# Seven more zero products on TensorE between the products of units 0 and 1

## The chip, the cores and the metric

The kernel runs on one core of one Trainium2 chip. Times are device microseconds of one execution; the time of a kernel is the median of its runs. The engines named here are TensorE (PE in the profile, with its weight loads as PEld), VectorE (DVE), ScalarE (ACT), GpSimd (POOL) and SyncE (SP), which issues nearly all DMAs.

## The reference

Two stages follow each other. The first is a linear attention with a decaying state, for 4 batches of 8 heads, 768 time steps and 48 channels:

```python
for t in range(S):
    cur = einsum('bhd,bhe->bhde', u[None] * kt, vt)
    y[:, :, t] = einsum('bhd,bhde->bhe', rt, state + cur)
    state = wt[:, :, :, None] * state + einsum('bhd,bhe->bhde', kt, vt)
```

The second mixes the tokens of each batch: with `x` the heads of `y` side by side (768 x 384), `wq = x @ w_q`, `wk = x @ w_k` (64 columns each), `W_tok = wq @ wk.T / 8`, and the output is `relu(W_tok @ x) @ w_out`.

## The kernel before, in words

The time axis is cut into units of 256 steps, two chunks of 128 each; 4 batches of 3 units make 12 units. For a unit the kernel loads w, k, r and v (each 384 KB; the v of the last batch in four pieces). GpSimd, ScalarE or VectorE cast them to bf16. ScalarE takes the logarithm of w (`lw`, line 407); TensorE sums it along time with a triangular matrix (`CM,lw`); ScalarE's exponentials of that are `ep` (447) and `en` (454). TensorE transposes k and r (`PM,k`, `PM,r`); VectorE or ScalarE copies the turned k as `ks`. VectorE and GpSimd form `RT` = r times ep (516), `KT` = k times en (521, 526) and `qT` = r times k (506). TensorE's `RT,KT` products are the scores within a chunk; VectorE masks them into `AM` (595). `UB,qT` gives the diagonal part, copied as `dd`, from which GpSimd forms `Vd` (575). `v,PM` puts v in order (copied as `VB`). KT is transposed back (`ID,KT`, copied as `kd`), and `VB,kd` with the old state through `SB,IDU` gives the next state, which VectorE scales into `SB` (658). `VB,AM` and `SB,RT` add up to y, which VectorE turns into `X` (710). The second stage's products (`XT`, `QK`, `TS`, `MX`, `wo`) follow at the end of each batch.

Nothing is scheduled by the compiler. The program first makes a list of steps (`Plan.add`), each a group of instructions on one engine, and then gives them out in the order of the list `ORDER` (lines 82 to 122), a permutation of the steps' numbers. `WAYS` names the engine where there is a choice, and `BANKS` (129) names the PSUM bank of each PSUM buffer, in the order in which the buffers are made. PSUM has eight banks, taken by many buffers in turn: a step that writes a bank must wait for the engines that last read it, and those waits follow from the order. Each engine takes its instructions strictly in the order of the list.

A zero product is a matmul of a tile of zeros, `Z` (128 x 512, set by line 250), with itself: a full-array product of 512 columns whose result nobody reads. Eighteen are issued at the start, while the first loads are on their way (251). Twelve more are steps of the plan, made at its end, each with a PSUM bank of its own from `BANKS`:

```python
for x in range(WARM):
    z = bank()
    add(("z", x), "E", lambda e, z=z: mm(at(z), Z[:, ds(0, C)], Z), [], z, [z])
```

All matmuls go through the helper `mm`, so that in the profile every TensorE instruction has its line, 179.

Of the kernel before, what the change touches and what calls it, by code (L numbers as in the profile page):

```python
# [32 lines left out]
class Plan:  # L33
# [47 lines left out]

ORDER = [
# [40 lines left out]
]  # L123
WAYS = (
    "PDDDAPPDDdPADPPDDEEEAAPPAdPAAPEAcEEAAPPAPPADPeDEEDAAAAAAAAPPDPDADPeAcEEDAPPAdPAAPEAEEEDA"
# [1 line left out]
    "DPPAPeAcceAAPPDPPPAPPAEEDDAEDADAAADAAAADADDA"  # L127
)
BANKS = [
# [6 lines left out]
]  # L136


WARM = 12


@with_exitstack
def kernel(
# [170 lines left out]
    def bank():  # L314
        return Buf("s")
# [537 lines left out]
    for n in range(N):  # L853
        if n % NU == 0:
            batch = {"k": [], "q": [], "x": []}
        unit(n, batch)
    for x in range(WARM):
        z = bank()
# [35 lines left out]
```

## Time and profile before

| | |
|---|---|
| median of 3 runs | 100.75 us (100.47 to 102.29) |
| profiled execution | 101.37 us |
| its span, first to last instruction | 99.6 us |
| TensorE busy | 86.6 us (87%), 1906 product rows |
| VectorE busy | 84.9 us (85%) |
| ScalarE busy | 79.0 us (79%) |
| GpSimd busy | 69.5 us (70%) |
| DMA | 24.68 MB, mean 248 GB/s |
| zero products | 8.4 us in 25 rows, of 30 issued |

The span is cut on the page into 40 slices of 2.5 us, with a digit for the busy share of each engine in tenths. The chain of waits goes back from the last instruction, at each step to what released it. Rows of a timeline join equal instructions that follow each other: start, length, engine, line, operation, output and inputs with their shapes, how many, and in brackets the idle time of the engine ahead of them and what ended it. A row's length goes from the first start to the last end; products are pipelined, so a following row can start before that end. Some product rows can be missing: five of the thirty zero products are.

### The profile page before, as it was taken

How to read it: one execution, taken by the hardware profiler on the slowest of the kernel's cores; microseconds unless marked ns; L12 is line 12 of the kernel's file. 1: busy time of each engine (PE TensorE's matmuls, PEld its weight loads, DVE VectorE, ACT ScalarE, POOL GpSimd, SP SyncE). 2: the span in 40 equal slices, each digit the busy share in tenths (PEclk: the TensorE clock that was granted, in tenths of full speed). 3: DMA queues.
4: the chain of work that ended last, by engine and by line, in shares of the span. 5: the costliest groups of instructions: out<-in, count | busy, mean ns of one | idle time of the engine just before them, and what ended most of it. 6: DMA issues, size and time to landing. Idle time of an engine off the chain costs nothing.

```text
span 99.6 us, 4492 instructions
## 1 busy us (share of the span) xinstructions
PE 86.6 (87%) x1906; PEld 63.3 (64%) x1911; DVE 84.9 (85%) x154; ACT 79.0 (79%) x135; POOL 69.5 (70%) x82
## 2 busy tenths in 40 slices
PE   5978796879886998999999999889998999999930
PEld 1325473756774767777776777759787687776610
DVE  6284999799979999979999999999999799783740
ACT  6034998799996799899999998999899766666920
POOL 6866354999799895799999989498996392500000
PEclk9999999999999999999999999999999999999999
DMA  1999999799999999999999977998993056030794
GB/s 17 313 327 349 324 337 296 195 295 335 289 314 298 225 311 329 344 321 268 271 330 305 316 114 218 251 156 201 282 417 115 7 210 264 10 158 7 277 367 149
DMA packets 45141, 24.68 MB, mean 248 GB/s; under 512 B 31552, under 2 KB 43968, under 8 KB 45120
## 3 DMA queue, kind: packets, MB, share of 16 engines
q1 hardware_dynamic: 44960, 24.19, 84.0%
q8 instruction: 15, 0.25, 0.9%
q10 hardware_dynamic: 160, 0.20, 0.5%
q14 instruction: 6, 0.05, 0.1%
HBM read 19.66 MB, written 4.72 MB: 245 GB/s over the span
## 4 chain that ended last, share of the span: by engine, by line
PE 37%; DVE 23%; SPq 20%; DMA 7%; issue 7%; ACT 3%; ACTq 0%; DVEq 0%
PE PS L179 37%; SPq L232 9%; SPq L237 8%; DMA vg<-in_v_dram 7%; DVE AM L595 7%; DVE X L710 6%; DVE RT L516 3%; SPq L355 2%; DVE qT L506 2%; DVE ks L333 2%; DVE SB L658 1%; ACT VB L327 1%; SPq L357 1%; ACT MX L339 1%; DVE kd L335 1%
## 5 line engine op out<-in xcount | busy, mean ns | idle before, releaser
L595 DVE TENSOR_TENSOR AM<-PS,US 128x1024 bf16<-128x1024 f32 x24 | 28.8, 1218 | 0.7 <-PE PS L179 0.7
L526 POOL TENSOR_TENSOR KT<-ks,en 128x1024 bf16<-128x1024 bf16 (+1 forms) x10 | 19.7, 1965 | 4.7 <-DVE ks L333 3.3
L575 POOL TENSOR_TENSOR Vd<-VB,dd 128x768 bf16<-128x768 bf16 (+1 forms) x14 | 18.1, 1293 | 4.5 <-ACT dd L327 3.4
L454 ACT ACTIVATE en<-PS 128x1024 bf16<-128x1024 f32 (+1 forms) x14 | 12.5, 907 | 3.0 <-PE PS L179 2.9
L179 PEld LDWEIGHTS <-KT 48*128 48x128 bf16 (+1 forms) x312 | 9.7, 94 | 6.6 <-issue 4.5
L447 ACT ACTIVATE ep<-PS 128x512 bf16<-128x512 f32 (+1 forms) x28 | 13.7, 555 | 0.1
L179 PE MATMUL PS<-wo,MX 128*128 128x384 bf16 x72 | 13.5, 327 | 0.0
L710 DVE SCALAR_TENSOR_TENSOR X<-PS,gx,Vd 128x384 bf16<-128x384 f32 x22 | 12.5, 609 | 0.7 <-PE PS L179 0.6
L407 ACT ACTIVATE lw<-wg 128x768 bf16<-128x768 f32 x12 | 10.3, 857 | 2.9 <-DMA wg<-in_w_dram 2.9
L179 PE MATMUL PS<-RT,KT 48*128 48x128 bf16 x192 | 9.7, 218 | 1.2 <-ACT VB L327 0.4
L327 ACT COPY os<-PS 128x768 f32<-128x768 f32 (+1 forms) x11 | 7.9, 714 | 3.5 <-PE PS L179 3.5
L418 POOL CAST k<-kg 128x768 bf16<-128x768 f32 x10 | 8.3, 827 | 2.5 <-DMA kg<-in_k_dram 2.5
L179 PE MATMUL PS<-Z 128*128 128x512 bf16 x25 | 8.4, 461 | 1.4 <-DVE Z L250 1.2
L418 POOL CAST r<-rg 128x768 bf16<-128x768 f32 x10 | 8.2, 825 | 1.6 <-DMA rg<-in_r_dram 1.6
L179 PEld LDWEIGHTS <-MX 128*128 128x128 bf16 x72 | 6.5, 97 | 3.6 <-DVE MX L341 0.2
L516 DVE TENSOR_TENSOR RT<-PS,ep 128x1024 bf16<-128x1024 bf16 (+1 forms) x14 | 8.4, 605 | 0.0
L179 PE MATMUL PS<-VB,AM 128*128 128x48 bf16 x192 | 8.0, 184 | 0.4 <-issue 0.4
L506 DVE TENSOR_TENSOR qT<-PS,ks 128x1024 bf16<-128x1024 bf16 x12 | 8.2, 684 | 0.1
L339 ACT ACTIVATE MX<-PS 128x768 bf16<-128x768 f32 (+1 forms) x12 | 8.0, 682 | 0.4
L179 PE MATMUL PS<-CM,lw 64*128 64x128 bf16 x192 | 7.4, 217 | 0.5 <-DVE AM L595 0.3
L327 ACT CAST VB<-PS 128x768 bf16<-128x768 f32 x8 | 6.4, 804 | 1.1 <-PE PS L179 0.6
L179 PEld LDWEIGHTS <-AM 128*128 128x128 bf16 x192 | 6.3, 96 | 1.6 <-issue 0.7
(90 smaller groups left out, 191.9 us busy)
## 6 DMA issues: line engine op xcount, KB each, us to landing
kg<-in_k_dram SPq DMA_DIRECT2D x12, 384.0 KB, 6.4
wg<-in_w_dram SPq DMA_DIRECT2D x12, 384.0 KB, 5.0
rg<-in_r_dram SPq DMA_DIRECT2D x12, 384.0 KB, 5.8
vg<-in_v_dram SPq DMA_DIRECT2D x9, 384.0 KB, 6.3
out_dram<-os SPq DMA_DIRECT2D x9, 384.0 KB, 2.5
vw<-in_v_dram SPq DMA_DIRECT2D x4, 288.0 KB, 6.7
out_dram<-os SPq DMA_DIRECT2D x5, 192.0 KB, 2.4
wof<-in_moe_w_out_dram SPq DMA_DIRECT2D x1, 576.0 KB, 6.2
```

What stands on the lines that cost most here:

```text
L179: return nc.tensor.matmul(o, l, rr, start=start, stop=stop, skip_group_check=True, is_transpose=trans)
L327: nc.scalar.copy(o, i)
L407: nc.scalar.activation(view(lw.tile, 0, [[64, H], [512, 2], [1, D]]), view(g["wg"].tile, 0, [[D2, H], [D, 2], [1, D]]), ACT.Ln, bias=0.0, ...
L418: op(view(o.tile, 0, [[64, NP], [256, 4], [1, D]]), view(g[src].tile, 0, [[2 * D2, NP], [D, 4], [1, D]]))
L447: nc.scalar.activation(view(ep.tile, cs[0] * NP * EW + off, [[EW, NP * len(cs)], [step, 2], [1, 32]]), view(at(cw), cs[0] * 512 + j * 64, ...
L454: nc.scalar.activation(en.tile[:, ds(cs[0] * 512, w_)], at(cw)[:, ds(cs[0] * 512, w_)], ACT.Exp, bias=0.0, scale=-1.0)
L506: lambda e: nc.vector.tensor_tensor(plain(qT.tile), turned(512), plain(ks.tile), ALU.mult),
L516: nc.vector.tensor_tensor(plain(RT.tile, cs, 32), turned(512, cs, True), plain(ep.tile, cs, EW // 4), ALU.mult)
L526: x.tensor_tensor(KT.tile[:, cols], ks.tile[:, cols], en.tile[:, cols], ALU.mult)
L575: (nc.vector if e == "D" else nc.gpsimd).tensor_tensor(Vd.tile[:, cols], VB.tile[:, cols], view(dd.tile, cs[0] * H, [[1, len(cs) * H], [0, ...
L595: AMs[c] = add(("AM", n, c), "D", lambda e, c=c, A=A: nc.vector.tensor_tensor(view(AM[c].tile, 0, [[C, 8], [1, C]]), view(at(A), 0, [[C, 8 ...
L710: nc.vector.scalar_tensor_tensor(view(X.tile, 2 * i * DM + hh * D, [[D2, H], [1, D]]), view(at(y), hh * 512, [[D, H], [1, D]]), gx, view(V ...
```

## The change

The number of zero products in the plan goes from 12 to 19. The seven new steps have the numbers 734 to 740; they are put into `ORDER` at five places between the products of units 0 and 1, and `BANKS` gets seven more entries, one for each: 4, 0, 0, 1, 0, 0, 2. The order of all other steps, their engines and their banks stay. The lists are written out with other line breaks, and the file is one line longer, so that a line of the kernel before has a number one higher in the changed one.

```diff
-    14, 30, 18, 19, 727, 79, 80, 81, 38, 33, 40, 32, 729, 82, 83, 84, 35, 731, 37, 39, 43, 726,
+    14, 30, 18, 19, 727, 79, 80, 81, 38, 33, 40, 32, 729, 82, 83, 84, 35, 731, 37, 39, 734, 43,
...
-WARM = 12
+WARM = 19
```

How TensorE's instructions stand, with the engine whose semaphore an instruction waits for: `LDWEIGHTS` loads the stationary operand, `MATMUL` is the product; the numbers in the names are those of the buffers (`_101` and `_99` are of unit 0, `_102` and `_100` of unit 1). First the end of unit 1's k transposes, unit 0's first score products and the first product with `qT`. Before:

```order
L179 LDWEIGHTS k_1_90
L179 MATMUL PS<-PM,k_1_90 128x2x32
L179 LDWEIGHTS KT_101 [waits DVE_49]
L179 MATMUL PS<-RT_99,KT_101 128x128 [waits Activation_49]
...
L179 LDWEIGHTS qT_97 [waits DVE_49]
L179 MATMUL PS<-UB,qT_97 128x2
```

The same place in the changed kernel:

```order
L180 LDWEIGHTS k_1_90
L180 MATMUL PS<-PM,k_1_90 128x2x32
L180 LDWEIGHTS Z
L180 MATMUL PS<-Z 128x512 [waits DVE_49]
L180 LDWEIGHTS Z
L180 MATMUL PS<-Z 128x512
L180 LDWEIGHTS KT_101
L180 MATMUL PS<-RT_99,KT_101 128x128 [waits Activation_49]
...
L180 LDWEIGHTS qT_97
L180 MATMUL PS<-UB,qT_97 128x2
```

Two zero products into bank 0 stand ahead of the score products. The first of them waits for VectorE, and neither the score products nor the products with `qT_97` do so any more: the wait of the latter has moved ahead of the former.

The second place is between unit 0's second score products and unit 1's first. Before:

```order
L179 LDWEIGHTS KT_101
L179 MATMUL PS<-RT_99,KT_101 128x128
L179 LDWEIGHTS Z
L179 MATMUL PS<-Z 128x512 [waits DVE_49]
L179 LDWEIGHTS Z
L179 MATMUL PS<-Z 128x512
L179 LDWEIGHTS KT_102 [waits DVE_49]
L179 MATMUL PS<-RT_100,KT_102 128x128 [waits Activation_49]
```

In the changed kernel:

```order
L180 LDWEIGHTS KT_101
L180 MATMUL PS<-RT_99,KT_101 128x128
L180 LDWEIGHTS Z
L180 MATMUL PS<-Z 128x512 [waits Activation_49]
L180 LDWEIGHTS Z
L180 MATMUL PS<-Z 128x512 [waits DVE_49]
L180 LDWEIGHTS Z
L180 MATMUL PS<-Z 128x512
L180 LDWEIGHTS Z
L180 MATMUL PS<-Z 128x512 [waits DVE_49]
L180 LDWEIGHTS KT_102
L180 MATMUL PS<-RT_100,KT_102 128x128
```

The first and the last of the four zero products are new, and they have taken over both waits of unit 1's score products.

The third place is ahead of the product that carries the state of unit 0 on. Before:

```order
L179 LDWEIGHTS r_1_88
L179 MATMUL PS<-PM,r_1_88 128x2x32
L179 LDWEIGHTS IDU
L179 MATMUL PS<-SB_115,IDU 128x192 [waits DVE_49]
L179 LDWEIGHTS kd_83
L179 MATMUL PS<-VB_105,kd_83 128x48
```

In the changed kernel:

```order
L180 LDWEIGHTS r_1_88
L180 MATMUL PS<-PM,r_1_88 128x2x32
L180 LDWEIGHTS Z
L180 MATMUL PS<-Z 128x512 [waits DVE_49]
L180 LDWEIGHTS IDU
L180 MATMUL PS<-SB_115,IDU 128x192
L180 LDWEIGHTS kd_83
L180 MATMUL PS<-VB_105,kd_83 128x48
```

The wait for VectorE has moved from that product to the zero product ahead of it. The remaining two new products wait for nothing: one beside the zero product that follows unit 0's r transposes, one ahead of unit 1's products with `qT_98`. The other engines' instructions stand as before.

89 rows, old and new, of tables (BANKS, ORDER) are left out of this document.

## The prediction

> **What bounds the kernel now.** I read the page first, then the chain of waits, then the timelines of TensorE, VectorE, ScalarE and GpSimd from 4 to 30 us, because all seven new products stand there. The two lines of the page are TensorE's granted clock in 40 slices and the chain's shares by engine; the rows under them are pieces of the chain (start, length, what).
>
> ```profile
> PEclk9999999999999999999999999999999999999999
> PE 37%; DVE 23%; SPq 20%; DMA 7%; issue 7%; ACT 3%; ACTq 0%; DVEq 0%
> ```
>
> ```profile
> 0.78 0.44 SPq L232
> ...
> 20.89 0.60 SPq L237
> 21.49 0.04 issue
> 21.53 7.07 DMA vg<-in_v_dram
> 28.60 0.02 issue
> 28.62 0.04 DVE v L333
> ```
>
> The clock is full in every slice. Up to 28.6 us the chain is not an engine at all: SyncE's load issues from 0.78 us on, and then the load of v for unit 3, issued at 21.53 and landed at 28.60. Only from 28.62 us on is it VectorE and TensorE that carry the end. The new products lie between 9.7 and 17.6 us, so the question is how late they make VectorE at 28.62 us, and whether any engine reaches that point late.
>
> The rows of TensorE around the seven places (start, length from the first start to the last end, product, how many; in brackets its idle time and what ended it):
>
> ```profile
> 1.23 3.57 PE L179 MATMUL PS<-Z 128*128 128x512 bf16 x8 [1.23 <-DVE Z L250]
> ```
>
> ```profile
> 4.62 2.34 PE L179 MATMUL PS<-Z 128*128 128x512 bf16 x10
> ```
>
> ```profile
> 9.74 0.39 PE L179 MATMUL PS<-Z 128*128 128x512 bf16 x1
> 10.32 0.60 PE L179 MATMUL PS<-ID,KT 48*128 48x48 bf16 x16 [0.20 <-DVE KT L526]
> 10.86 0.36 PE L179 MATMUL PS<-v,PM 64*64 64x384 bf16 x4
> 11.15 0.52 PE L179 MATMUL PS<-PM,k 64*128 64x64 bf16 x16
> 12.12 0.40 PE L179 MATMUL PS<-RT,KT 48*128 48x128 bf16 x8 [0.45 <-ACT VB L327]
> 12.45 0.35 PE L179 MATMUL PS<-UB,qT 128*128 128x2 bf16 x8
> 12.66 0.36 PE L179 MATMUL PS<-VB,kd 128*128 128x48 bf16 x8
> 12.95 0.62 PE L179 MATMUL PS<-CM,lw 64*128 64x128 bf16 x16
> 13.76 0.41 PE L179 MATMUL PS<-PM,r 64*128 64x64 bf16 x16 [0.19 <-ACT ks L327]
> 14.16 0.24 PE L179 MATMUL PS<-SB,IDU 128*128 128x192 bf16 x1
> 14.25 0.36 PE L179 MATMUL PS<-VB,kd 128*128 128x48 bf16 x8
> 14.45 0.38 PE L179 MATMUL PS<-Z 128*128 128x512 bf16 x1
> 14.76 0.36 PE L179 MATMUL PS<-v,PM 64*64 64x384 bf16 x4
> 15.04 0.35 PE L179 MATMUL PS<-UB,qT 128*128 128x2 bf16 x8
> 15.68 0.40 PE L179 MATMUL PS<-RT,KT 48*128 48x128 bf16 x8 [0.28 <-ACT dd L327]
> 16.01 0.39 PE L179 MATMUL PS<-Z 128*128 128x512 bf16 x1
> 16.55 0.40 PE L179 MATMUL PS<-RT,KT 48*128 48x128 bf16 x8
> 17.52 0.26 PE L179 MATMUL PS<-PM,k 64*128 64x64 bf16 x6 [0.57 <-POOL k L418]
> ```
>
> **What one zero product costs.** Ten follow each other from 4.62 us: (2.34 - 0.39) / 9 = 0.22 us each, where 0.39 is one's own length (row at 16.01). The eight before them took (4.62 - 1.23) / 8 = 0.42 each, at the lower clock. One that is followed by products of another tile shape delays them by 0.31 (14.45 to 14.76, and 15.68 + 0.33 = 16.01 for what precedes it). So I take 0.22 when a full-array product follows, 0.31 when a narrower one does; the bounds are 0.22 and 0.39 (no overlap at all with what follows).
>
> **The seven, one after the other.** The releasing rows on VectorE, ScalarE and GpSimd:
>
> ```profile
> 10.98 0.68 DVE L506 TENSOR_TENSOR qT<-PS,ks 128x1024 bf16<-128x1024 bf16 x1
> ...
> 12.62 1.22 DVE L595 TENSOR_TENSOR AM<-PS,US 128x1024 bf16<-128x1024 f32 x1
> 13.77 0.35 DVE L658 TENSOR_TENSOR SB<-PS,ep 128x192 bf16<-128x192 f32 x1
> ...
> 15.75 0.68 DVE L516 TENSOR_TENSOR RT<-PS,ep 128x1024 bf16<-128x1024 bf16 x1
> 16.35 2.35 DVE L595 TENSOR_TENSOR AM<-PS,US 128x1024 bf16<-128x1024 f32 x2
> 19.32 1.14 DVE L710 SCALAR_TENSOR_TENSOR X<-PS,gx,Vd 128x384 bf16<-128x384 f32 x2 [0.62 <-PE PS L179]
> ```
>
> ```profile
> 14.54 1.09 ACT L447 ACTIVATE ep<-PS 128x512 bf16<-128x512 f32 x2
> 15.50 0.19 ACT L327 COPY dd<-PS 128x16 f32<-128x16 f32 x1
> ```
>
> ```profile
> 16.64 0.82 POOL L418 CAST k<-kg 128x768 bf16<-128x768 f32 x1 [1.47 <-DMA kg<-in_k_dram]
> ```
>
> ```profile
> 28.62 1.31 DVE L333 CAST v<-vg 128x768 bf16<-128x768 f32 x1 [0.73 <-DMA vg<-in_v_dram]
> ```
>
> Product 1 stands beside the zero product at 9.74. The two take 0.22 + 0.31, so the transposes of KT can start at 10.27; they wait for KT until 10.32 anyway. Cost 0.
>
> Products 2 and 3 stand ahead of unit 0's first RT,KT products (12.12), in an idle gap of 0.45. But they write bank 0, which VectorE's qT reads until 10.98 + 0.68 = 11.66; the wait that the later UB,qT products had has moved up to product 2. A release takes about 0.05 (ep ends at 14.54 + 1.09 = 15.63, the RT,KT products that need it start at 15.68): start 11.71, then 0.22 + 0.31, and RT,KT at 12.24 in place of 12.12: +0.12. VectorE's first mask product AM follows, 12.74 for 12.62, and ScalarE's en (which waits for CM,lw) is 0.12 late too. The r transposes at 13.76 wait for ScalarE's ks, and stay.
>
> Product 4 waits for the same SB as the SB,IDU product behind it (SB ends 13.77 + 0.35 + 0.12 = 14.24). It starts at 14.29, SB,IDU at 14.51: +0.35. It fills no wait, it stands after one. The VB,kd products behind it end at 14.25 + 0.36 + 0.35 = 14.96, VectorE's next SB follows at 15.01, about 0.12 late, and so does all of VectorE's row up to the AM at 16.35.
>
> Product 5 stands ahead of UB,qT (15.04) and waits for nothing: 0.35 + 0.22 = +0.57, at 15.61. ScalarE's dd follows UB,qT's end: 15.61 + 0.35 + 0.05 = 16.01, done at 16.20. RT,KT of unit 0's second chunk has cover here, the wait for ep (14.54 + 1.09 = 15.63): 15.61 + 0.21 (12.45 to 12.66) + 0.1 for the change of shape (0.31 against 0.22) = 15.92 for 15.68, +0.24.
>
> Products 6 and 7 stand around the two zero products from 16.01 (one row of the two is missing in the trace). Product 6 waits for that dd: 16.25. The two old ones follow at 16.47 and 16.69, product 7 at 16.91 (it waits for RT, which ends at 15.75 + 0.68 + 0.12 = 16.55), and RT,KT of unit 1 at 17.22 for 16.55: **+0.67**, the largest lag of TensorE. Its AM, second of the pair at 16.35, starts at 17.22 + 0.40 + 0.05 = 17.67 for 16.35 + 2.35 - 1.22 = 17.48: +0.19 on VectorE.
>
> **Where it is taken back.** Three idle times stand behind this. TensorE's next work, the k transposes at 17.52, waits for GpSimd's cast, which itself waited 1.47 us for a DMA (16.64 + 0.82 = 17.46): TensorE is free again at 17.22 + 0.33 = 17.55, so 0.67 shrinks to 0.03. VectorE idles 0.62 before X at 19.32, which waits for TensorE: the 0.19 is gone. And at 28.62 VectorE idles 0.73 for the load of v. Between 0.78 and that load's issue at 21.53 the chain holds nothing but issues of loads, no engine, so a lag of some tenths on an engine moves none of it. Sum on the path: 0.00 to 0.05 us. Against the profiled execution (99.6 us span, 101.37 us in all, 1.77 outside) that is 101.4; the median of the runs shown is 100.75, 0.62 lower, so 100.8 on that scale.
>
> If every zero product cost its whole 0.39 with nothing overlapped, the same walk gives RT,KT of unit 1 at about 18.1, k transposes at 18.46 (+0.94) and X at 20.3 (+0.94 on VectorE); the 0.73 at 28.62 leaves 0.2 to 0.3. That is the upper end of the working: 101.05.
>
> **A gain?** The stretch itself, by a view of engines in windows (busy, instructions, granted clock, DMA share, GB/s):
>
> ```profile
> 13.40:16.80 3.40, 2.78 (x63) 1.79 (x56) 3.31 (x8) 3.40 (x7) 1.16 (x3) 1.00 1.11 324
> ```
>
> TensorE has the full clock here, and the longest idle time in the rows above is 0.57. Zero products could only raise a clock that is low; by these rows their gain is 0. [...]
>
> **Rivals.** (1) *The clock falls in executions other than the profiled one, and the new products hold it.* For it: the three runs lie between 100.47 and 102.29, wide for one kernel. Against it: full clock in all 40 slices. Price: a low stretch as long as the first one (1.23 to 4.62, 3.4 us) does half the work; of 2.78 us busy it does 1.70, so TensorE falls back by 1.08. The idle times of 0.62 and 0.73 take 1.35, so one such stretch costs nothing at the end; two cost 2.16 - 1.35 = 0.81. The change would win that: 99.9. Chance 0.10. [...]
>
> (2) *The lag gets past the covers (slower).* Place: VectorE's X at 19.32 and its cast at 28.62. It decides once VectorE is over 0.62 late before X and over 0.73 late at the cast. Against it: by the walk above it is 0.19 late. For it: behind X VectorE has no idle time that would take a lag back (third pair of the row: busy 5.00 of 5.00 us),
>
> ```profile
> 20.00:25.00 5.00, 4.14 (x102) 3.11 (x103) 5.00 (x9) 4.84 (x9) 4.92 (x4) 1.00 1.04 316
> ```
>
> so what X brings stays, up to 25 us at the least. Price +0.2 to +0.3: 101.05. Chance 0.15. At the far end of the same rival nothing covers, and 7 x 0.31 = 2.2 us come out at the end: 102.95; chance 0.04 of its own, since it needs the load of v to move with the engines.
>
> (3) The forecast, within 0.1 of 100.8: 0.71.
>
> **How the numbers follow.** Likeliest case: 100.8. A measurement of this kernel can tell about 2% from no change: below 98.7 or above 102.8. No case with a price lies below 98.7; I leave 0.03 there for rival 1 at more than two low stretches, and 0.05 above 102.8, for the far end of rival 2 and the spread of the runs. Same: 0.92. For the range, the cases' prices (99.9 to 101.05) are widened by half the spread of the runs shown, (102.29 - 100.47) / 2 = 0.91, on the upper side, where a median of few runs can fall: 101.05 + 0.91, about 102.0. Below, the lowest price and the median less that spread agree (99.9 and 99.84): 99.8.
>
> **What would show it.** In the changed kernel's timelines: the first RT,KT near 12.25; SB,IDU near 14.5; the second UB,qT near 15.6; unit 1's first RT,KT near 17.2; then k transposes still near 17.5, X near 19.3 with its idle time cut from 0.62 to about 0.4, and the cast of v at 28.6 still behind a DMA with about 0.7 idle. Wrong are the steps if X comes after 19.6, wrong is the cover if the cast waits for an engine, and wrong is the whole forecast if the load of v lands at another time or a slice of the clock falls below 9.

## The result, and the profile after

| | kernel before | changed kernel |
|---|---|---|
| median, 6 executions each | 100.69 us (100.21 to 102.29) | 102.32 us (101.69 to 103.01) |
| ratio, 95% interval | | 1.0146 (1.0097 to 1.0194) |
| profiled execution, its span | 101.37, 99.6 us | 101.69, 100.0 us |

By the medians the changed kernel is 1.6 us slower; by the two profiled executions 0.3 us. The profiled execution of the changed kernel is its fastest, that of the kernel before slower than five of its six others. Ratios here and below leave out disturbed executions, while the medians are over all, so that the two need not agree.

First the clock and the chain's shares on the page of the changed kernel:

```profile
PEclk9999999999999999999999999999999999999999
PE 49%; DVE 17%; DMA 8%; POOL 8%; issue 8%; ACT 5%; SPq 1%; DVEq 0%; ACTq 0%; POOLq 0%
```

The clock is full, as before. The first 28 us of the chain are no longer SyncE's issues: the 20% of SPq have gone to engines, TensorE first. The timeline of TensorE at the new products (start, length, product, count):

```profile
12.20 0.40 PE L180 MATMUL PS<-RT,KT 48*128 48x128 bf16 x8
14.47 0.24 PE L180 MATMUL PS<-SB,IDU 128*128 128x192 bf16 x1
15.57 0.34 PE L180 MATMUL PS<-UB,qT 128*128 128x2 bf16 x8
16.18 1.04 PE L180 MATMUL PS<-Z 128*128 128x512 bf16 x4
17.15 0.40 PE L180 MATMUL PS<-RT,KT 48*128 48x128 bf16 x8
17.39 0.41 PE L180 MATMUL PS<-PM,k 64*128 64x64 bf16 x16
```

and VectorE's X and cast of v:

```profile
19.18 1.14 DVE L711 SCALAR_TENSOR_TENSOR X<-PS,gx,Vd 128x384 bf16<-128x384 f32 x2 [0.29 <-PE PS L180]
28.40 0.73 DVE L334 CAST v<-vg 128x768 bf16<-128x768 f32 x1 [0.64 <-DMA vg<-in_v_dram]
```

Every place stands within 0.07 us of the forecast (12.24, 14.51, 15.61, 17.22), and both covers are there: the k transposes start at 17.39, not later than before, X keeps 0.29 us of its idle time, and the cast of v still waits for its load, 0.64 us. X and the cast are even 0.14 and 0.22 us earlier than before. The local walk holds; what the profiled execution lost it lost later. From 30 to 67 us VectorE is 0.8 to 1.1 us ahead of before (the cast of v took 0.73 us, 1.31 before); then ScalarE waits for a load. SyncE's issues and ScalarE's logarithm of w for unit 10 in the changed kernel:

```profile
57.84 1.52 SPq L233 DMA_DIRECT2D wg<-in_w_dram  x1
65.77 0.84 ACT L408 ACTIVATE lw<-wg 128x768 bf16<-128x768 f32 x1 [1.01 <-DMA wg<-in_w_dram]
```

and in the kernel before:

```profile
58.74 1.25 SPq L232 DMA_DIRECT2D wg<-in_w_dram  x1
65.42 0.88 ACT L407 ACTIVATE lw<-wg 128x768 bf16<-128x768 f32 x1
```

The load was issued 0.9 us earlier and came 1.7 us later (landing 65.69 for 64.00). So the lead of 0.8 us was lost to a load, and VectorE was 0.18 us late behind it; a longer wait of TensorE near 77 us (rows below) made it 0.37, and so it stayed to the end. That accounts for the profiled pair. It doesn't explain 1.6 us between the medians, and the experiments are about that.

### The profile page after: what moved, and what is told of

It is laid out like the page before. It is cut to its first block, busy times and chain, and to the rows that moved or that the text cites. A ratio compares the mean times of both kernels' runs of the same rounds, so it can differ in the third digit from the quotient of the medians.

```text
span 100.0 us, 4511 instructions
## 1 busy us (share of the span) xinstructions
PE 88.7 (89%) x1918; PEld 63.7 (64%) x1918; DVE 84.7 (85%) x154; ACT 79.2 (79%) x135; POOL 70.1 (70%) x82
## 4 chain that ended last, share of the span: by engine, by line
PE 49%; DVE 17%; DMA 8%; POOL 8%; issue 8%; ACT 5%; SPq 1%; DVEq 0%; ACTq 0%; POOLq 0%
PE PS L180 49%; DMA wg<-in_w_dram 8%; DVE X L711 5%; DVE AM L596 5%; ACT ep L448 2%; POOL KT L527 2%; POOL v L334 2%; ACT en L455 1%; DVE qT L507 1%; DVE ks L334 1%; DVE kd L299 1%; POOL US L287 1%; POOL CM L269 1%; DVE SB L659 1%; ACT lw L408 1%
## 5 line engine op out<-in xcount | busy, mean ns | idle before, releaser
L180 PE MATMUL PS<-Z 128*128 128x512 bf16 x37 | 12.3, 445 | 1.3 <-DVE Z L251 1.2
L334 DVE COPY ks<-PS 128x1024 bf16<-128x1024 bf16 x8 | 5.5, 685 | 2.3 <-PE PS L180 2.3
L180 PEld LDWEIGHTS <-Z 128*128 128x128 bf16 x37 | 3.8, 111 | 5.7 <-issue 3.0
```

What stands on the lines that cost most here:

```text
L180: return nc.tensor.matmul(o, l, rr, start=start, stop=stop, skip_group_check=True, is_transpose=trans)
L334: x.tensor_copy(o, i)
```

## The experiments

Five comparisons, each on one chip with 18 to 36 executions of the kernel before. Beside the ratio, executions are sorted by their mean granted clock: "full" is 0.99 or more.

**First comparison: parts of the change.** The kernel before on this chip: 102.47 us, 36 executions, the clock under 0.99 in 23.

A copy of the kernel before, for the size of a difference that means nothing (edit: one blank line).

> The kernel before with one blank line more, so the same instructions. Both theories expect a ratio of 1.000 within 0.003. It says how far two equal programs lie apart, which the 1.5% of the change has to be seen against; and it gives a second trace of the kernel before, in which the load of w for the last unit is expected to land near 64 us, as in the first one (64.0), and not near 65.7 as in the changed kernel.

102.75 us, ratio 0.9957 (0.9902 to 1.0012). The clock was under 0.99 in 6 of 12, so falls of the clock belong to the program as it was. In the copy's trace the load of w for unit 10, expected near 64 us, landed at 65.90: a late landing isn't the changed kernel's alone.

The seven new products with 8 columns in place of 512:

```diff
+        w_ = 512 if x < 12 else 8
-        add(("z", x), "E", lambda e, z=z: mm(at(z), Z[:, ds(0, C)], Z), [], z, [z])
+        add(("z", x), "E", lambda e, z=z, w_=w_: mm(at(z)[:, ds(0, w_)], Z[:, ds(0, C)],
+                                                    Z[:, ds(0, w_)]), [], z, [z])
```

> The seven new products stand where they stand in the changed kernel, with their waits and weight loads, but with 8 columns in place of 512. Theory A (TensorE's time: the 0.2 to 0.3 us of each new product are what costs) expects nearly the time of before, under +0.4 us. Theory B (the instructions: 14 more of them in TensorE's stream move the places where it stands still for its code) expects the loss to stay, +1.2 to +2.0 us. Theory C (the load stream is what the kernel hangs on, and any small change of the early timing shifts it) expects some other amount, 0 to +1.6.

101.92 us, 0.994 (0.9889 to 0.9991); clock under 0.99 in 7 of 12.

Products 1 to 3 alone, then 4 to 7 alone (the other numbers taken out of `ORDER`; `WARM` is 15 and 16, here the first):

```diff
-WARM = 19
+WARM = 15
```

> Only the first three of the seven new products (the one beside the zero product after the r transposes, the two ahead of unit 0's first score products). Theory A: under half of the loss, 0 to +0.5 us, since only 0.1 us of lag comes from these. Theory B: about three sevenths of it or all of it, by the places of the stalls. Theory C: anything between 0 and +1.6, and not the difference to the run with the other four.

> Only the last four of the seven new products (ahead of SB,IDU, ahead of unit 1's products with qT, and the two ahead of unit 1's score products). Theory A: nearly the whole loss, +1.0 to +1.6 us, since the 0.67 us of lag at unit 1's score products comes from these. Theory B: about four sevenths or all. Theory C: anything, and the sum with the run of the first three need not give +1.6.

The first three: 101.62 us, 0.9969 (0.9926 to 1.0012), clock under 0.99 in 1 of 12. The last four: 101.87 us, 0.9973 (0.9922 to 1.0023), 5 of 12. No part gives anything like 1.5%: theory B misses with the products of 8 columns, theory A with the last four. But the clock does fall in executions of the kernel before, as rival 1 had it. The granted clock of the unchanged copy's profiled execution, and its stretch of 3.4 us (busy times and counts of PE, PEld, DVE, ACT, POOL; clock; DMA share; GB/s):

```profile
PEclk9999967999999999589999999999999999999999
13.25:16.65 3.40, 3.40 (x62) 2.51 (x62) 3.07 (x7) 2.88 (x6) 1.69 (x3) 0.50 1.08 323
```

Half speed from 13.23 to 16.64 us, where the forecast's row for the kernel before had 1.00, and once more from 40.53. Its X still comes at 19.38 us (19.32 in the full-clock execution): one stretch here is covered, as rival 1 priced it.

**Second comparison: the changed kernel again, fewer loads, no zero products.** The kernel before: 102.64 us, 29 executions, 21 under 0.99.

> The changed kernel once more, beside the kernel before on one chip. Three theories stand. Products: the seven new products themselves cost TensorE and VectorE time that comes out at the end; then the ratio is again near 1.015 (1.010 to 1.019) at any chip. Loads: the local work keeps its covers, and what made the changed kernel 1.5% slower is when the loads of unit 10 land (w at 65.69 us in the changed kernel's trace, at 64.00 in that of before), which differs from execution to execution; then the ratio is between 0.99 and 1.005, and the profiled span goes with the landing of w of unit 10: near 99.5 if it lands before 64.5, near 100 to 101 if it lands after 65.5. Clock: the new products keep TensorE's clock from falling (6 of 6 executions of the changed kernel at 0.994 or more, 23 of 36 of the kernel before below 0.99 in the first comparison); then no more than 2 of its executions are below 0.99, and the ratio is 0.98 to 1.00 wherever the kernel before falls.

101.86 us, ratio 1.0002 (0.9947 to 1.0057), clock under 0.99 in 3 of 12. The 1.5% didn't come back.

The loads of v for units 4 to 8 left out of the kernel before, and of the changed kernel (these units then compute with old data):

```diff
+            skip = name == "vg" and n >= 4
-            g[name + "L"] = dma((name, n), lambda e, ap=ap, f=f, x=g[name].tile: f(b, i, x, ap),
+            g[name + "L"] = dma((name, n), lambda e, ap=ap, f=f, x=g[name].tile, skip=skip:
+                                None if skip else f(b, i, x, ap), buf=g[name])
```

> The kernel before without the loads of v for units 4 to 8 (the casts then read v of earlier units, so these units' outputs are wrong by that); 5 of 48 loads and 1.9 MB less, some 6.5 us of the loads' time. Loads: r and w of unit 10 land some 5 us earlier than 62.08 and 64.00, ScalarE's lw of unit 10 waits for no DMA, and the time is 0 to 1 us less than before, with a narrower spread. Products: nothing changes, ratio 0.995 to 1.005.

> The changed kernel with the same loads of v left out (units 4 to 8 read v of earlier units). To be set against the kernel before with the same loads left out. Loads: with the loads of unit 10 out of the way the two are equal within 0.5%. Products: the changed one is 1.0 to 1.9% slower than its counterpart, as it was with all loads.

100.28 us, 0.9865 (0.9816 to 0.9913), and 101.39 us, 0.9984 (0.994 to 1.0028), of the kernel before with all loads. Against each other 1.1%: the load theory, which expected them equal, was wrong, or something else lay in between. The fall of 1.4% for the kernel before is more than the 0 to 1 us that it allowed.

The twelve zero products of the plan taken out:

```diff
-WARM = 12
+WARM = 0
```

> The kernel before without its own twelve zero products in the plan (the eighteen at the start stay). Clock: the clock falls in nearly every execution (11 or 12 of 12 below 0.99, against about two thirds of those of the kernel before), over a longer stretch after 13 us, and the time is 1 to 3 us more. Products: twelve products of 0.22 to 0.39 us less, so 0 to 1 us faster. Loads: between 0.99 and 1.01.

106.2 us, 1.0304 (1.0187 to 1.0421), under 0.99 in 6 of 6, half speed from 13.11 to 30.18 us:

```profile
PEclk9999955555579957999999999999999999999995
```

So what the twelve zero products do in this kernel is to hold the clock, and that is worth 3 to 4 us (106.2 for 102.64).

**What makes the executions differ at the full clock.** The page of the kernel before had "issue 7%" in its chain, and the forecast passed over it. Of these 6.8 us most stand ahead of VectorE's, SyncE's and ScalarE's instructions; 1.2 us are TensorE waiting for nothing that the profile shows. TensorE's waits of this kind come to 1.6 us in all, and but for two of 0.15 and 0.16 us they stand at fixed places. Counting products from 0, these are among the numbers 96, 224, 352 and so on, every 128th; with its weight load each product is two instructions (the page counts 1906 products and 1911 weight loads), so every 256 instructions. The page has a queue of instructions (packets, MB, share):

```profile
q8 instruction: 15, 0.25, 0.9%
```

15 packets of 16 KB, as many as there are such places, 96 to 1888. From these counts the author takes each packet for the next block of 256 instructions of TensorE, and these places for the blocks' edges; no row names what a packet holds. Edge 1632 in the kernel before:

```profile
76.54 0.29 PE L179 MATMUL PS<-PM,k 64*128 64x64 bf16 x8
77.34 0.29 PE L179 MATMUL PS<-PM,k 64*128 64x64 bf16 x8 [0.51 <-issue]
```

and in the changed kernel:

```profile
76.72 0.20 PE L180 MATMUL PS<-PM,k 64*128 64x64 bf16 x1
77.61 0.39 PE L180 MATMUL PS<-PM,k 64*128 64x64 bf16 x15 [0.69 <-issue]
```

The same edge stands after 8 of the 16 transposes before, after 1 of them now: seven products earlier in the work, by the seven that were put in ahead. So the change does a second thing that the forecast didn't see: it moves the later block edges. Where TensorE waited at such an edge, in any of the traces, it went on 1.2 to 1.7 us after the last packet had arrived (at edge 1632 the packets arrived at 76.01 us before and at 76.44 us now).

**Third comparison: are the moved edges what costs?** The kernel before: 102.21 us, 35 executions, 18 under 0.99. The two kernels without v again, and between them the kernel before without v, with seven products of 8 columns at the start, which move the edges by as much and put nothing between units 0 and 1:

```diff
         for _ in range(18):
             mm(PS[:, ds(0, 512)], Z[:, ds(0, C)], Z)
+        for _ in range(7):
+            mm(PS[:, ds(0, 8)], Z[:, ds(0, C)], Z[:, ds(0, 8)])
```

> The kernel before without the loads of v for units 4 to 8 (wrong in these units by that), once more, as the base of the next two. If its 100.28 us against 102.64 for the kernel before was the loads' doing, it is again 1 to 2% faster than the kernel before. Code theory: TensorE's instructions arrive in blocks of 128 products, the block edges show as waits for nothing at products 480, 736, 864, 992, 1248 and 1632 of the traces so far, 0.3 to 1.5 us each, ended 1.3 to 1.6 us after a packet of 16 KB; such a packet is late when loads are in its way. Then this kernel's sum of such waits is under 1.2 us.

> The changed kernel without the same loads of v. The first pair gave 101.39 against 100.28, 1.1% more, where the load theory expected no difference. Products: again 0.7 to 1.5% more than its counterpart. Code: the same, by block edges that lie 7 products earlier in the work. Chance: within 0.5%.

> The kernel before without the same loads of v, with seven products of 8 columns more at the very start, behind the eighteen zero products of the start: they move every block edge of TensorE's code 7 products earlier in the work, as the seven new products do, and put nothing between units 0 and 1. Code: as the changed kernel without these loads, within 0.5% of it, and 0.7 to 1.5% slower than its counterpart. Products: as the kernel before without these loads, within 0.4%. Chance: all three alike.

> The changed kernel with all loads on another occasion. If the 1.5% of the first comparison belongs to the change, the ratio is 1.010 to 1.019; by the second comparison, with both kernels' executions at the full clock only, 0.995 to 1.007. Clock: no more than 4 of its executions under 0.99, more than half of those of the kernel before.

Before without v: 101.28 us, 0.9974 (0.9914 to 1.0034), with the clock low in 10 of 12 (1 to 2% under the kernel before was expected); the changed kernel without v: 100.84 us, 0.9924 (0.9865 to 0.9983), low in 1; the shift without v: 100.71 us, 0.9955 (0.9895 to 1.0015), low in 1. As medians the order of the first pair is turned round, by the clock. At the full clock, both occasions together, they are 100.07, 101.05 and 100.73 us (standard errors 0.13, 0.17, 0.21). The shift alone lies two thirds of the way to the changed kernel, against the products theory, though this rests on 9, 21 and 11 executions that the clock has picked. TensorE around 50 us in the changed kernel without v, first occasion:

```profile
50.22 0.36 PE L180 MATMUL PS<-PM,r 64*128 64x64 bf16 x13 [0.62 <-issue]
```

second occasion:

```profile
50.24 0.36 PE L180 MATMUL PS<-PM,r 64*128 64x64 bf16 x13 [0.64 <-issue]
```

and in the shift:

```profile
50.26 0.36 PE L179 MATMUL PS<-PM,r 64*128 64x64 bf16 x13 [0.64 <-issue]
```

The same wait at the same product (992); of the two traces of the kernel before without v one has 0.15 us there, in its weight loads, and one none. And a wait can make all the difference between two executions of one kernel. The changed kernel without v near 66 us, first occasion (span 98.7 us):

```profile
66.28 0.62 PE L180 MATMUL PS<-CM,lw 64*128 64x128 bf16 x16
```

second occasion (span 100.0 us):

```profile
66.32 0.56 PE L180 MATMUL PS<-CM,lw 64*128 64x128 bf16 x13
68.02 0.27 PE L180 MATMUL PS<-CM,lw 64*128 64x128 bf16 x3 [1.14 <-issue]
```

At 66.3 us the two are level within 0.04 us; one waits at edge 1376, and the spans end 1.3 us apart.

The changed kernel with all loads: 102.19 us, 1.0035 (0.9986 to 1.0083), under 0.99 in 4 of 12.

**Fourth comparison: with all loads.** The kernel before: 102.07 us, 35 executions, 16 under 0.99. The shift by seven and by three with all loads, the changed kernel a third time, the first three products again.

> The kernel before with all its loads and seven products of 8 columns at the start, behind the eighteen zero products: TensorE's code has its block edges where the changed kernel has them, and nothing new stands between units 0 and 1. Code: at the full clock it is as the changed kernel of the same call, within 0.4%, and its waits at block edges are the same ones (736, 992, 1248, 1376 by turns). Products: as the kernel before at the full clock, within 0.3%, while the changed kernel is above both. Clock: without these loads the same shift brought executions below 0.99 from 10 of 12 to 1 of 12; if that holds, no more than 3 of 12 here, and the median is 0.5 to 1% under that of the kernel before.

> As the last, with three such products at the start, so that the block edges lie 3 products earlier. Code: between the kernel before and the shift by seven, all within 0.5% at the full clock. Clock: if these products hold it by their mere presence, no more than 3 of 12 executions below 0.99; if it goes by how many they are, about half.

> The changed kernel a third time beside the kernel before. At the full clock 0.995 to 1.007 of it if the 1.5% belonged to one occasion; 1.010 to 1.019 if that chip is met again and the two later ones were the exceptions. No more than 4 of 12 executions below 0.99.

> Products 1 to 3 alone, once more, as the version that might beat both: 101.62 us against 102.47 with the clock low in 1 of 12 executions. Clock: again no more than 3 of 12 below 0.99 and a median 0.5 to 1% under the kernel before. Chance: within 0.3% of it.

Shift by seven: 102.48 us, 1.0049 (0.9966 to 1.0133), low in 8 of 12. By three: 101.97 us, 1.0036 (0.9988 to 1.0085), low in 7 of 13. The changed kernel: 101.52 us, 0.998 (0.9932 to 1.0029), low in 1 of 12. The first three: 102.95 us, 0.9981 (0.9911 to 1.0052), low in 3. With all loads moved edges cost nothing that shows, though with four and six executions at the full clock (table below) several tenths of a microsecond could hide. That products at the start hold the clock, as it seemed without v, was wrong. The first three alone didn't beat the kernel before a second time.

**Fifth comparison: the loads out of the way.** The kernel before: 102.24 us, 18 executions, 13 under 0.99. Neither w, k, r nor v is loaded for units 4 to 8:

```diff
-            skip = name == "vg" and n >= 4
+            skip = 4 <= n <= 8
```

> The kernel before without any load of w, k, r and v for units 4 to 8 (their casts read data of earlier units, so these units' outputs are wrong by that): 7.5 MB less, next to nothing to load between about 31 us and the end of unit 8. If the code packets of TensorE are late because loads are in their way, the waits for nothing at products 480 to 1120 shrink to under 0.3 us in sum (1.0 to 2.7 us in an execution with all loads), and the full-clock time is 0.5 to 1.5 us under the 100.07 us that the kernel before took without v alone. If loads have nothing to do with them, they stay at 1 to 2 us.

> The changed kernel without the same loads. With the waits at the block edges gone, what is left between this and its counterpart at the full clock is what the seven products cost by themselves: by the forecast's walk 0 to 0.05 us where the load of v for unit 3 still covers them, 0.1 to 0.4 us where it does not. If instead they cost 1 us by themselves, as the pairs without v read at the full clock (101.05 against 100.07), that stays. Clock: no more than 4 of 12 below 0.99, half or more for its counterpart.

The kernel before with few loads: 100.15 us, 0.9857 (0.9786 to 0.9928), 6 executions, low in 4; the changed kernel: 100.64 us, 0.9955 (0.9897 to 1.0013), 12 executions, low in 1. TensorE's waits for nothing, in all, how often, the longest, in the kernel before with few loads:

```profile
PE PS L179 <- issue: 0.2, 1, 0.2
```

and in the kernel before with all loads:

```profile
PE PS L179 <- issue: 1.6, 6, 0.5
```

The waits at the edges are gone (the 0.2 us stand elsewhere, at 9.04 us), as expected if loads are what makes the code late. The packets show it too: the six that follow edges 480 to 1120 start 1.0 us after the edge in the median, against 2.9 us in the kernel before with all loads. It isn't the loads alone: the kernel without its twelve zero products has all of them, these packets start after 1.5 us there, and it has no such wait. The spread of the kernel before nearly goes as well: 99.96 to 100.20 us in five of six executions (one at 101.39). But the time didn't fall as expected: 0.5 to 1.5 us under the 100.07 us without v were forecast, and 100.15 us came.

The profiled pair differs by 0.7 us of span, and not by the products. TensorE's k transposes and VectorE's X before (few loads):

```profile
17.34 0.41 PE L179 MATMUL PS<-PM,k 64*128 64x64 bf16 x16 [0.20 <-POOL k L419]
19.13 1.14 DVE L711 SCALAR_TENSOR_TENSOR X<-PS,gx,Vd 128x384 bf16<-128x384 f32 x2 [0.24 <-PE PS L179]
```

and in the changed kernel (few loads), with the row of unit 1's RT,KT products and GpSimd's cast of k:

```profile
17.02 0.82 POOL L420 CAST k<-kg 128x768 bf16<-128x768 f32 x1 [1.51 <-DMA kg<-in_k_dram]
17.40 0.40 PE L180 MATMUL PS<-RT,KT 48*128 48x128 bf16 x8
17.90 0.41 PE L180 MATMUL PS<-PM,k 64*128 64x64 bf16 x16
19.69 1.14 DVE L712 SCALAR_TENSOR_TENSOR X<-PS,gx,Vd 128x384 bf16<-128x384 f32 x2 [0.56 <-PE PS L180]
```

X follows the k transposes by 1.79 us in both (1.80 and 1.79 in the two kernels with all loads). The transposes wait for the cast of k, done at 17.02 + 0.82 = 17.84, and that for a load that landed at 16.87 us here, 16.31 there: 0.56 us, and X is 0.56 us later. TensorE was free of RT,KT at 17.40 + 0.24 = 17.64, ahead of the cast. The load had been issued at 9.66 us, before any new product ran. After this VectorE's rows stay 0.55 to 0.56 us apart up to 69 us; a wait of 0.3 us at edge 1376, in the weight loads, adds the rest. In this pair of traces the seven by themselves cost what the forecast said. Of the twelve executions of the changed kernel six lie at 100.19 to 100.33, about 0.1 us above the five of the kernel before; the other six lie between 100.61 and 101.67. Of these only the profiled one (100.80) has a trace; why the rest are longer isn't shown.

**All executions with all loads,** the comparison of the result left out:

| kernel | executions | clock under 0.99 | mean at the full clock (standard error, count) |
|---|---|---|---|
| before, and its copy | 165 | 97 | 101.68 (0.08, 68) |
| seven products | 36 | 8 | 101.64 (0.13, 28) |
| first three | 24 | 4 | 101.83 (0.19, 20) |
| last four | 12 | 5 | 101.44 (0.18, 7) |
| seven of 8 columns | 12 | 7 | 101.68 (0.32, 5) |
| shift by seven | 12 | 8 | 101.59 (0.39, 4) |
| shift by three | 13 | 7 | 101.73 (0.24, 6) |

At the full clock the change costs -0.04 us, with a standard error of 0.15. With the result's executions counted in (those of the kernel before taken as full, their clocks not being on record) it is +0.16, with the same error. Under 0.99 the kernel before takes 103.00 us in the mean, 1.3 more.

## Why the prediction was right and wrong

*The walk over the seven products* was right, place by place, to 0.07 us, and in the profiled execution so was where it is taken back: the k transposes wait for the cast of k, and X follows them by 1.79 us. The sum of 0.00 to 0.05 us agrees with three comparisons (1.0002, 1.0035, 0.998) and with -0.04 us at the full clock, none of which could tell 0.2 us from it.

*The cover at 17.5 us* isn't there in every execution. In two of the seven traces with all seven products the load of k landed early, at 16.16 and 16.31 us, and the k transposes follow unit 1's RT,KT products, 0.25 to 0.27 us behind the end of the cast, not 0.05 to 0.06. The changed kernel's third run, whose cast of k ended at 17.29:

```profile
17.30 0.40 PE L177 MATMUL PS<-RT,KT 48*128 48x128 bf16 x8
17.54 0.40 PE L177 MATMUL PS<-PM,k 64*128 64x64 bf16 x16
19.32 1.14 DVE L708 SCALAR_TENSOR_TENSOR X<-PS,gx,Vd 128x384 bf16<-128x384 f32 x2 [0.28 <-PE PS L177]
27.82 1.45 DVE L331 CAST v<-vg 128x768 bf16<-128x768 f32 x1
```

In the kernel before with few loads the same load also landed at 16.31; X came at 19.13 and the cast of v, which waits for no load in either, at 27.63. So in such an execution the seven make VectorE 0.19 us late, and the lag lasts to the cast at least.

*The cover at 28.62 us* was read as the kernel's. It was that execution's: in 17 of the 20 traces, few loads and low clocks among them, the cast of v for unit 3 waits for no load; it does in the two traces of the result and in the shift by three. In the six others with all loads and the clock full so far, v landed at 27.0 to 27.5 us and the cast stood at 27.7 to 27.9. The forecast survived this since at most 0.2 us was left to cover there. But the page's chain, 28 us of SyncE and a load, wasn't the chain of the usual execution.

*The time and the range* were wrong: 102.32 us against 99.8 to 102.0. The step that failed, as far as the runs show, is the last of the sum, "the median of the runs shown is 100.75, 0.62 lower, so 100.8 on that scale", with the 0.91 added to the range. It took three executions for the kernel's scale. At the full clock the kernel before averages 101.68 us and the changed one 101.64: of the 1.5 us between 100.8 and 102.32 this accounts for 0.8 (100.8 to 101.64), and 0.7 stays open (below). The kernel before spreads from 100.3 to 103.2 us at the full clock. The chief causes that the traces show are the waits at block edges (1.0 to 2.7 us of "issue" in TensorE's waits per full-clock execution with all loads), which its views already had, and when single loads land (0.56 us by one load of k, a wait of 1.0 by one of w), which one execution can't show. Nor did the working look past 28 us, and there lies all that the changed kernel lost in the profiled pair.

*Rival 1, the clock,* had 0.10 and deserved more. "Full clock in all 40 slices" was one execution; 97 of 165 show it lower. (The row has 9 even for the first 4.6 us, where the forecast found zero products at half the rate, 0.42 us each for 0.22, and put it down to a lower clock: the view of 1.20 to 4.60 us has a granted clock of 1.00, so that isn't shown.) That one stretch costs next to nothing was right where the trace shows it; two in a row put X at 20.64 and 21.02 us in two traces, 1.3 and 1.7 late, where its working gives 2.16 - 0.62 = 1.54. That the new products hold the clock is borne out: low in 8 of 36, and in 4 of 24 with the first three alone, but in 7 of 12 when they have only 8 columns. In five traces the clock falls between 13.07 and 13.84 us, in none of the nine with the first three products at full width. That points to what they add to TensorE's work from 9.7 to 12.2 us; how they do it isn't shown. It isn't all that matters: without v the kernel before was low in 14 of 23 and the shift, with nothing new there, in 1 of 12, which stays unexplained. The three later medians of the changed kernel are 0.78, 0.02 and 0.55 us under those of the kernel before, as rival 1 would have it, but no ratio shows a gain.

*Rival 2, the lag past the covers,* is there at its small end: 0.19 us in the execution above, by its price 0.2 to 0.3, though not by its condition, since nothing was 0.62 us late before X. It isn't what made the 1.6 us of the result, whose profiled pair has X 0.14 us early.

*What stays open* is the comparison of the result itself. Both of its sides are unusual: five of the kernel before's six executions lie under 100.8 us, where 6 of 68 full-clock ones do elsewhere, so on that occasion the scale of 100.75 did hold for it; and the changed kernel's average 102.34, 0.7 above its others. Without v, where the kernel before also ran near 100 us, the changed kernel was 1 us slower at the full clock and the shift alone 0.7; so moved edges may have cost as much there. That is argued, not shown: no execution of it but the profiled two has a trace, and the three further comparisons with all loads didn't bring it back. Which loads delay which packet wasn't tried one by one.

## What to carry to other kernels

A cover seen in one profile may belong to that execution: ask whether the row that ends last waits for a load, and how far that load's landing moves between executions, before a sum is set against a median of three. Seven products put into this kernel's TensorE program moved the later block edges by seven products, and with all loads TensorE waited at such edges, up to 1.6 us at one of them; look at the waits that the profile ends with "issue". The clock was full in the profile of the kernel before, and under 0.99 in 97 of 165 later executions of it and its copy: sort executions by granted clock first.

## What the runs showed of the hardware

- TensorE's waits for nothing at the block edges, 256 instructions apart, were 0.16 to 1.63 us long and ended 1.2 to 1.7 us after a packet of 16 KB had arrived; in the trace of the kernel before with few loads no edge has such a wait. Spans at the full clock went with the sum of TensorE's waits for nothing: 98.5, 98.7, 100.0, 100.2 us for 1.0, 1.3, 1.9, 2.6 us without v; 99.0, 99.6, 99.7, 99.9, 100.4 for 1.2, 1.6, 1.7, 1.9, 2.7 with all loads (off this line lie 100.0 for 1.0, the changed kernel with its late load of w, and 99.4 for 1.8).
- The clock fell to half for 3.41 us (13.23 to 16.64 in the copy of the kernel before), 6.83 or 17.07 us (13.11 to 30.18 without the twelve zero products), one, two and five times the same length. The idle time ahead didn't tell whether it would fall: ahead of the fall at 13.23 us the longest idle time of TensorE in 7 us was 0.56 us, and ahead of three later falls (at 39.9, 40.53 and 33.98 us) 1.35, 1.63 and 1.64 us. The first two of these idle times are waits at edge 736. An idle time of 1.45 us at the same edge in the first three's trace was followed by no fall.
- Twelve zero products of 0.22 to 0.31 us each were worth 3 to 4 us to this kernel: without them it took 106.2 us for 102.64, with the clock at half for 17.07 us.
